# Attention and rational feed-forward on one core: float32 products with undivided w_out in the first twelve units, w_out divided later, denominators added by GpSimd throughout

## The chip, the cores and the metric

The kernel runs on one core of one Trainium2 chip. The metric is device time in microseconds of one execution, measured over several runs; one further execution was recorded by the hardware profiler. The engines are called as the profile calls them: PE (TensorE matmuls), PEld (its weight loads), DVE (VectorE), ACT (ScalarE), POOL (GpSimd), SP (SyncE, which issues the transfers).

## The reference

```python
# q, k, v: 8 x 8 x 576 x 64; p: 8 x 8 x 32 x 64 (batch, head, row, head_dim)
def sm_attn(qq, kk, vv):
    s = scale * np.matmul(qq, kk.transpose(0, 1, 3, 2))
    s = s - np.max(s, axis=-1, keepdims=True)
    a = np.exp(s)
    a = a / (np.sum(a, axis=-1, keepdims=True) + 1e-09)
    return np.matmul(a, vv)
p_packed = sm_attn(p, k, v)
x = sm_attn(q, p_packed, p_packed)      # then to 4608 rows of 512 = 8 heads x 64
# w_in: 512 x 2048, w_out: 2048 x 512, both given in float64; a: 4, b: 2 numbers
h = x @ w_in
P = a[0] + a[1] * h + a[2] * h2 + a[3] * h3
Q = 1.0 + np.abs(b[0]) * np.abs(h) + np.abs(b[1]) * h2
g = P / (Q + 1e-6)
out = (g @ w_out).astype(np.float32)    # 4608 x 512
```

## The kernel before

**Units.** The feed-forward part runs in 128 units: 8 batches, two halves `x` of a batch's 576 rows, and 8 chunks `c` of 256 of the 2048 hidden columns. `hidden(bb, x, c)` makes a unit's hidden values in two halves `f` of 128 columns: six matmuls into an `h` bank, then the numerator `Y` (ACT, then two instructions of DVE), the denominator `U`, its reciprocal by Ln and Exp on ACT and a correction on DVE, and the quotient `g` in `Y`. It is a generator with four parts, and step `u` of the main loop runs the first two parts of unit `u`, the last of unit `u-2` and the third of unit `u-1`. The rows of a half are 256 (`HMAIN`, multiplied unit by unit) and 32, which are gathered in `G` and multiplied by `remainder` for two batches together.

**Exactness by division.** Matmuls of full speed take `fp32r` operands, which hold fewer bits than float32. So `split` divides a float32 operand into a rounded part (an ACT cast, `gh`) and the rest (a POOL subtraction, `gl`), and a product is three matmuls: `gh` by `wh`, `gh` by `wl`, `gl` by `wh`, in `accumulate`. `acc_block(u, i)` multiplies a unit's 128-row part `i` by the chunk's two rows of w_out and adds it up in a PSUM bank over the eight chunks: 12 matmuls of 512 columns for a unit. It is called at step `u + 3` (`LAG`).

**Words.** w_in and w_out come as 64-bit words of float64. `load_words` brings a chunk into a free buffer (`room` lists the buffers and up to which word they may be used), and `convert` makes float32 of it: two ACT instructions and three on DVE (a mask by `TENSOR_SCALAR`, a shift by `SCALAR_TENSOR_TENSOR`, a 32-bit sum, which the profile calls `CUSTOM_DVE_ANT_0`). A chunk of w_out is then divided by `split` into `W[c]`, kept in the ring `w`: eight buffers of 8 KB in each partition, four parts of 512 columns each. The last chunk of w_out comes in two halves through the buffers `o` and `full`. Four words are converted before the main loop, then at least one in each step, so that `converted < len(words)` holds for units 0 to 9.

**Denominators.** While words are left (`early`), the denominator is made by ACT (`Abs`), DVE (a second product by `h`) and ACT again (`Abs` of the whole); later ACT makes `Abs` and `Square` (into `sq`, a ring of one buffer), and POOL adds the two.

**Order.** `Planner` records every operation with its engine and operands, finds the dependences, prices each operation (a float32 matmul at 30 ns and 1.667 ns a column, an fp32r one at 15 and 0.417), and issues all of them in the order of a list schedule. `idle` puts small matmuls on a zero tile between PE's operations, where that schedule leaves PE idle in its first 150 us; they add zeros to a sum that is open. In the profile all operations of the schedule have line 226, the zero matmuls line 223; so the tiles' names tell the operations apart. The next batch's `attention` and `m_chunk` (the packed keys times w_in) are spread over the steps as fillers.

Of the kernel before, what the change touches and what calls it, by code (L numbers as in the profile page):

```python
# [23 lines left out]
P = 128  # L24
# [233 lines left out]
def attention_rational_ffn(  # L258
# [46 lines left out]

    w_ring = Ring(sb, "w", NCH, [P, 2, 2, DM], F32R)
    o_ring = Ring(sb, "o", 1, [P, 2, DM])

# [51 lines left out]

    words = [("in", 2 * c, 2) for c in range(NCH)] + [("out", 2 * c, 2) for c in range(NCH - 1)]
    words += [("out", NFC - 2 + i, 1) for i in range(2)]
    due = lambda x: x[1] // 2 + (LAG if x[0] == "out" else -2)
# [3 lines left out]
    room = [((m_ring, i), index["in", 4 * i] + 1) for i in range(NCH // 2)]  # L367
    room += [((w_ring, c), index["out", 2 * c]) for c in range(1, NCH)]
    started = False
    words_in, converted = [], 0  # L370

    def load_words(n):
        while len(words_in) < min(len(words), converted + n):
            r = len(words_in)
            kind, i, n2 = words[r]
            used = [x for x, _ in words_in]
            free = [x for x, end in room if r < end and x not in used[converted:]]
            free = [x for x in free if x[0] is not w_ring or x[1] < NCH - 2 or started]
            if not free and r == converted and n2 == 1:
                free = [(o_ring, 0)]  # L380
            if not free:
                return
            x = min(free, key=lambda x: max((j for j in range(r) if used[j] == x), default=-1))
            raw = x[0].at(x[1], [P, n2 * 512], I64)
            if kind == "in":
                c = i // 2
                for y in range(2):
                    src = w_in[2 * y * P : (2 * y + 2) * P, c * CF : (c + 1) * CF].rearrange("(x p) f -> p x f", p=P)
                    nc.sync.dma_start(raw[:, 512 * y : 512 * (y + 1)].rearrange("p (x y) -> p x y", x=2), src)
            else:  # L390
                for y in range(n2):
                    nc.sync.dma_start(raw[:, 512 * y : 512 * (y + 1)], w_out[(i + y) * P : (i + y + 1) * P, :])
            words_in.append((x, raw))

    W = {}

# [4 lines left out]
    def convert():  # L401
# [9 lines left out]
        if kind == "in":  # L411
            dst = win[:, i // 2]
            di = dst.bitcast(I32)
        else:
            dst = lo.bitcast(F32)
            di = w_ring.at(i // 2, [P, n * DM], I32) if n == 2 else full_ring.next(dtype=I32)
            di = di.rearrange("p (x y) -> p x y", x=n)
        nc.scalar.activation(hi.bitcast(F32), hi.bitcast(F32), AF.Copy, scale=REBIAS)
# [4 lines left out]
        nc.vector.tensor_add(dst.bitcast(I32), hi, di)  # L423
        if kind == "out":
            if i // 2 not in W:
                W[i // 2] = w_ring.at(i // 2)
            for y in range(n):
                split(dst[:, y, :], *(W[i // 2][:, (i + y) % 2, x, :] for x in range(2)))
        converted += 1
# [14 lines left out]
    def load(bb, what):  # L444
# [43 lines left out]
        if bb == 0 and x != "k":  # L488
            if g == 0:
                NAT[x] = w_ring.at(NCH - 2 + "vq".index(x), [P, 2, 4 * NS * D], F32)  # L490
            t = NAT[x][:, g, :]
        else:
            t = nat_ring.next()[:, 0 : 4 * NS * D]
# [283 lines left out]

    def hidden(bb, x, c):
        ah, al = AH[bb], AL[bb]
        mh, ml = (M[bb, c // 2][:, i, :, c % 2 * CF : (c % 2 + 1) * CF] for i in range(2))  # L780
        early = converted < len(words)
        U, V, Y = U_ring.next(), V_ring.next()[:, :, 0:HALF], Y_ring.next()
        U2 = None if early else U2_ring.next()
        for f in range(2):
# [8 lines left out]
            nc.scalar.activation(y, h, AF.Identity, scale=reg_a3, bias=a2)  # L793
            nc.scalar.activation(u, h, AF.Abs, scale=reg_b1 if early else reg_b0)
            if not early:
                nc.scalar.activation(U2[:, f, :], h, AF.Square, scale=reg_root)
            nc.vector.tensor_mul(y, y, h)
            nc.vector.scalar_tensor_tensor(y, y, a1, h, ALU.add, ALU.mult)


            if early:
                nc.vector.scalar_tensor_tensor(u, u, b0, h, ALU.add, ALU.mult)
            elif f == 1:
                nc.gpsimd.tensor_add(U, U, U2)
            yield
        if early:
            nc.scalar.activation(U, U, AF.Abs)
        nc.scalar.activation(V, U, AF.Ln, bias=one)
        nc.scalar.activation(V, V, AF.Exp, scale=-1.0)
        nc.vector.scalar_tensor_tensor(Y, Y, a0, V, ALU.add, ALU.mult)  # L810
        nc.vector.scalar_tensor_tensor(V, U, (1.0 + 1e-6) * S, V, ALU.add, ALU.mult)
        yield
        nc.vector.scalar_tensor_tensor(Y, V, 2.0, Y, ALU.subtract, ALU.mult, reverse0=True)
        gh, gl = GS[bb, x, c] = gh_ring.next(), gl_ring.next()
        split(Y[:, :, 0:HMAIN], gh, gl)
        r0 = (bb % 2) * REM + x * HREM
        nc.gpsimd.tensor_copy(G[:, 2 * c : 2 * c + 2, r0 : r0 + HREM], Y[:, :, HMAIN:HALF])
        yield

    def accumulate(acc, gh, gl, fc, first, last):  # L820
        wh, wl = (W[fc // 2][:, fc % 2, x, :] for x in range(2))
        for i, (x, w) in enumerate(((gh, wh), (gh, wl), (gl, wh))):
            nc.tensor.matmul(acc, x, w, start=first and i == 0, stop=last and i == 2)
# [3 lines left out]
    def remainder(bb, f4):  # L827

        full = G[:, 4 * f4 : 4 * f4 + 4, :].rearrange("p a b -> p (a b)")
        gx = o_ring.next(dtype=F32R)  # L830
        gh, gl = gx[:, 0, :], gx[:, 1, :]
# [23 lines left out]
    def acc_block(u, i):  # L855
        bb, x, c = units[u]
        if c == 0 and i == 0:
            ACC[bb, x] = [acc_ring.next() for _ in range(2)]
        gh, gl = GS[bb, x, c]
        acc = ACC[bb, x][i]  # L860
        for f in range(2):
            cols = slice(i * P, (i + 1) * P)
            accumulate(acc, gh[:, f, cols], gl[:, f, cols], 2 * c + f, c == 0 and f == 0, c == NCH - 1 and f == 1)
        if c < NCH - 1:
            return
        if i == 0:
            O[bb, x] = o_ring.next()
        o = O[bb, x]
# [52 lines left out]
    for u in range(NU + LAG + 2):  # L921
# [23 lines left out]
    def idle(i, t0, t1):  # L945
# [47 lines left out]
```

## Time and profile before

| | us |
|---|---|
| median of the runs (lowest, highest of 3) | 802.2 (801.95, 803.88) |
| the profiled execution, its own time | 802.42 |
| its span, from first to last instruction | 800.6 |
| PE busy | 751.5 (94%) |
| DVE busy | 707.2 (88%) |
| ACT busy | 670.5 (84%) |
| POOL busy | 460.5 (58%) |

A share of busy time is an average over the whole span. The page also divides the span into 40 equal slices of 20 us, and any stretch can be asked for by itself. A group's row names the operation, the tiles it writes and reads, its shape and count, then busy microseconds, the mean of one in ns, and the idle time of the engine before it with what ended that. Matmuls overlap one another, so the mean of one is longer than its share of PE's time; how far apart they start tells the latter.

### The profile page before, as it was taken

What the parts mean: (1) busy time and instruction counts of PE and PEld (TensorE: products, weight loads), DVE (VectorE), ACT (ScalarE), POOL (GpSimd) and SP (SyncE); (2) the same over time, 40 slices, a digit from 0 to 9 for tenths busy, and PEclk for the clock granted to TensorE, in tenths of its full rate; (3) what the DMA queues carried; (4) which work ended last, traced back from release to release, by engine and by line L of the source; (5) the groups of instructions that cost most, each with busy time, mean ns of one, the idle gap of its engine ahead of it and who ended that gap; (6) DMA issues with size and microseconds to landing.
All of it is one profiled execution on the core that took longest, in us unless ns stands there. A gap on an engine that the chain in (4) does not pass through costs nothing.

```text
span 800.6 us, 15433 instructions
## 1 busy us (share of the span) xinstructions
PE 751.5 (94%) x5537; PEld 593.6 (74%) x5537; DVE 707.2 (88%) x1309; ACT 670.5 (84%) x1494; POOL 460.5 (58%) x462
## 2 busy tenths in 40 slices
PE   2767989999999999999999999999999999999997
PEld 1446667778878788778877888778877887778886
DVE  4599999998899799998899789998899789998883
ACT  4699989889888898889888798889788798998972
POOL 0003547755577555756568455855578555866663
PEclk9958999999999999999999999999999999999999
DMA  7983236010651109120720219020810123000001
GB/s 249 365 272 108 89 105 86 27 57 27 76 78 43 40 15 124 30 57 28 105 48 3 81 25 133 11 57 28 116 37 28 53 41 60 1 1 27 27 1 40
DMA packets 152029, 56.05 MB, mean 70 GB/s; under 512 B 122256, under 2 KB 141200, under 8 KB 151952
## 3 DMA queue, kind: packets, MB, share of 16 engines
q1 hardware_dynamic: 151952, 55.07, 30.4%
q8 instruction: 43, 0.70, 0.4%
q14 instruction: 34, 0.28, 0.1%
HBM read 45.62 MB, written 9.44 MB: 69 GB/s over the span
## 4 chain that ended last, share of the span: by engine, by line
PE 73%; DVE 14%; ACT 8%; issue 2%; DMA 2%; SPq 1%; POOL 0%; DVEq 0%; ACTq 0%
PE acc L226 37%; PE h L226 23%; PE at L226 13%; DVE Y L226 5%; DVE w L226 3%; DMA nat<-in_k_dram 2%; ACT Y L226 2%; DVE small L226 1%; ACT U L226 1%; DVE kx L226 1%; ACT V L226 1%; ACT sq L226 1%; DVE V L226 1%; ACT kx L226 1%; DVE win L226 1%
## 5 line engine op out<-in xcount | busy, mean ns | idle before, releaser
L226 PE MATMUL acc<-w,gh 128*128 128x512 f32 x1024 | 324.2, 399 | 3.8 <-ACT gh L226 2.2
L226 PEld LDWEIGHTS acc<-w,gh 128*128 128x128 f32 x1024 | 184.3, 188 | 53.8 <-issue 7.5
L226 POOL TENSOR_TENSOR U<-U,sq 128x576 f32<-128x576 f32 x118 | 168.9, 1431 | 82.1 <-ACT U L226 48.7
L226 PE MATMUL h<-AH,m 128*128 128x288 f32 x1024 | 189.0, 304 | 10.6 <-DVE Y L226 8.0
L226 POOL TENSOR_TENSOR gl<-Y,gh 128x512 fp32r<-128x512 f32 x128 | 165.9, 1296 | 50.1 <-ACT gh L226 22.2
L226 PE MATMUL acc<-w,gl 128*128 128x512 f32 x512 | 191.3, 396 | 0.0
L226 PEld LDWEIGHTS h<-AH,m 128*128 128x128 f32 x1024 | 158.2, 190 | 39.7 <-DVE Y L226 24.2
L226 ACT ACTIVATE Y<-h,abS 128x288 f32<-128x288 f32 x256 | 125.6, 508 | 17.8 <-PE h L226 13.3
L226 ACT ACTIVATE sq<-h 128x288 f32<-128x288 f32 x236 | 97.5, 415 | 41.0 <-PE h L226 31.8
L226 DVE TENSOR_TENSOR Y<-Y,h 128x288 f32<-128x288 f32 x256 | 109.5, 444 | 25.0 <-ACT Y L226 9.3
L226 DVE SCALAR_TENSOR_TENSOR Y<-Y,abS,h 128x288 f32<-128x288 f32 x256 | 124.8, 504 | 2.3
L226 DVE SCALAR_TENSOR_TENSOR Y<-Y,abS,V 128x576 f32<-128x576 f32 x128 | 102.9, 804 | 21.9 <-ACT V L226 21.5
L226 PEld LDWEIGHTS acc<-w,gl 128*128 128x128 f32 x512 | 96.0, 188 | 27.3 <-issue 8.0
L226 PE MATMUL h<-AL,m 128*128 128x288 f32 x512 | 110.9, 297 | 0.0
L226 ACT ACTIVATE U<-h 128x288 f32<-128x288 f32 x256 | 98.6, 420 | 11.1 <-DVE V L226 5.7
L226 ACT ACTIVATE V<-U,one 128x576 f32<-128x576 f32 x128 | 98.0, 765 | 6.4 <-DVE Y L226 6.2
L226 POOL COPY G<-Y 128x64 f32<-128x64 f32 x128 | 34.3, 268 | 115.8 <-DVE Y L226 103.3
L226 DVE SCALAR_TENSOR_TENSOR Y<-V,Y 128x576 f32<-128x576 f32 x128 | 95.4, 746 | 1.9
L226 DVE SCALAR_TENSOR_TENSOR V<-U,V 128x576 f32<-128x576 f32 x128 | 96.0, 750 | 0.0
L226 ACT CAST gh<-Y 128x512 fp32r<-128x512 f32 x128 | 81.0, 633 | 6.0 <-DVE Y L226 5.3
L226 ACT ACTIVATE V<-V 128x576 f32<-128x576 f32 x128 | 84.6, 661 | 0.5
L226 PEld LDWEIGHTS h<-AL,m 128*128 128x128 f32 x512 | 83.0, 190 | 0.1
(127 smaller groups left out, 856.2 us busy)
## 6 DMA issues: line engine op xcount, KB each, us to landing
out_dram<-o SPq DMA_DIRECT2D x15, 512.0 KB, 2.8
w<-in_moe_w_out_dram SPq DMA_DIRECT2D x14, 512.0 KB, 4.4
nat<-in_k_dram SPq DMA_DIRECT2D x48, 144.0 KB, 3.9
nat<-in_q_dram SPq DMA_DIRECT2D x48, 144.0 KB, 4.2
nat<-in_v_dram SPq DMA_DIRECT2D x24, 256.0 KB, 4.0
m<-in_moe_w_in_dram SPq DMA_DIRECT2D x8, 512.0 KB, 7.5
w<-in_moe_w_in_dram SPq DMA_DIRECT2D x8, 512.0 KB, 9.7
nat<-in_k_dram SPq DMA_DIRECT2D x4, 512.0 KB, 11.1
```

Source lines behind the costliest of these rows:

```text
L226: getattr(getattr(self.nc, engine), name)(*args, **kwargs)
```

## The change

Four things are changed.

- The first twelve units (`PLAIN`) multiply in float32: `g` isn't divided, it is written by DVE as float32, the 256 rows into a buffer of `gh` or `gl`, and the 32 straight into `G`; and `acc_block` makes four float32 matmuls by the undivided chunk `X[c]` instead of twelve. These are all eight chunks of the first half of batch 0 and four of the second.
- `convert` leaves a chunk of w_out undivided, in `X[c]`. `divide(c)` makes `W[c]` of it by one ACT cast of 1024 columns and two POOL subtractions, at steps 11, 12, 14, 15, 17, 18, 20 and 21.
- All units make the denominator by `Abs` and `Square` on ACT and a POOL addition.
- The buffers: `w` has six instead of eight, a ring `half` of five buffers of 4 KB takes undivided chunks 2 and 3, two divided ones and what was `o`; raw words use `m0` to `m3` and `w1` to `w5`; batch 0's `v` and `q` lie in `w2` and `w3` instead of `w6` and `w7`. The last chunk of w_out comes as one word like the others.

```diff
+    PLAIN = 12
+    UNDIVIDED = {0: (0, 1), 4: (4, 5), 5: (6, 7)}
+    DIVIDE = dict(zip((11, 12, 14, 15, 17, 18, 20, 21), (4, 5, 6, 7, 0, 1, 2, 3)))
+    DIVIDED = {4: 1, 5: 2, 6: 3, 7: 4, 0: 5, 1: (2, 3), 2: 0, 3: (0, 4)}
...
-    w_ring = Ring(sb, "w", NCH, [P, 2, 2, DM], F32R)
-    o_ring = Ring(sb, "o", 1, [P, 2, DM])
+    w_ring = Ring(sb, "w", NCH - 2, [P, 2, 2, DM], F32R)
+    half_ring = Ring(sb, "half", 5, [P, 2, DM])
...
-    words = [("in", 2 * c, 2) for c in range(NCH)] + [("out", 2 * c, 2) for c in range(NCH - 1)]
-    words += [("out", NFC - 2 + i, 1) for i in range(2)]
+    words = [(kind, 2 * c, 2) for kind in ("in", "out") for c in range(NCH)]
...
-    room += [((w_ring, c), index["out", 2 * c]) for c in range(1, NCH)]
+    room += [((w_ring, i), len(words)) for i in (1, 2, 3)]
+    room += [((w_ring, i), index["out", 2 * UNDIVIDED[i][0]]) for i in (4, 5)]
...
+    def divide(c):
+        place = DIVIDED[c]
+        if isinstance(place, int):
+            t = w_ring.at(place)
+            hi, lo = W[c] = t[:, 0], t[:, 1]
+        else:
+            hi, lo = W[c] = [half_ring.at(i, dtype=F32R) for i in place]
+        nc.scalar.copy(hi, X[c])
+        for f in range(2):
+            nc.gpsimd.tensor_sub(lo[:, f], X[c][:, f], hi[:, f].bitcast(F32))
+
+    def o_next(dtype=None):
+        return half_ring.at(1 if 3 in W else 4, dtype=dtype)
...
-            dst = lo.bitcast(F32)
-            di = w_ring.at(i // 2, [P, n * DM], I32) if n == 2 else full_ring.next(dtype=I32)
-            di = di.rearrange("p (x y) -> p x y", x=n)
+            dst = undivided(i // 2)
+            di = dst.bitcast(I32)
...
-        if kind == "out":
-            if i // 2 not in W:
-                W[i // 2] = w_ring.at(i // 2)
-            for y in range(n):
-                split(dst[:, y, :], *(W[i // 2][:, (i + y) % 2, x, :] for x in range(2)))
...
     def hidden(bb, x, c):
+        plain = (2 * bb + x) * NCH + c < PLAIN
...
-        early = converted < len(words)
-        U2 = None if early else U2_ring.next()
+        U2 = U2_ring.next()
...
-            nc.scalar.activation(u, h, AF.Abs, scale=reg_b1 if early else reg_b0)
-            if not early:
-                nc.scalar.activation(U2[:, f, :], h, AF.Square, scale=reg_root)
+            nc.scalar.activation(u, h, AF.Abs, scale=reg_b0)
+            nc.scalar.activation(U2[:, f, :], h, AF.Square, scale=reg_root)
...
-            if early:
-                nc.vector.scalar_tensor_tensor(u, u, b0, h, ALU.add, ALU.mult)
-            elif f == 1:
+            if f == 1:
                 nc.gpsimd.tensor_add(U, U, U2)
             yield
-        if early:
-            nc.scalar.activation(U, U, AF.Abs)
...
+        r0 = (bb % 2) * REM + x * HREM
+        if plain:
+            g = GS[bb, x, c] = (gh_ring if c % 2 == 0 else gl_ring).at(c // 2 % 2, dtype=F32)
+            for o, cols in ((g, slice(0, HMAIN)), (G[:, 2 * c : 2 * c + 2, r0 : r0 + HREM], slice(HMAIN, HALF))):
+                nc.vector.scalar_tensor_tensor(
+                    o, V[:, :, cols], 2.0, Y[:, :, cols], ALU.subtract, ALU.mult, reverse0=True
+                )
+            yield
+            return
...
     def acc_block(u, i):
...
+        if u < PLAIN:
+            for f in range(2):
+                g = GS[bb, x, c][:, f, cols]
+                nc.tensor.matmul(acc, g, X[c][:, f, :], start=c == 0 and f == 0, stop=c == NCH - 1 and f == 1)
+        else:
+            gh, gl = GS[bb, x, c]
+        for f in range(0 if u < PLAIN else 2):
             accumulate(acc, gh[:, f, cols], gl[:, f, cols], 2 * c + f, c == 0 and f == 0, c == NCH - 1 and f == 1)
...
+        if u in DIVIDE:
+            divide(DIVIDE[u])
...
-                n = min(args[0].shape[-1], 256)
+                n = min(args[0].shape[-1], 256 if args[1].dtype == F32R else 96)
```

More of the change, by code (lines that the diff above doesn't have):

```diff
@@ L377, in load_words @@
             free = [x for x, end in room if r < end and x not in used[converted:]]
-            free = [x for x in free if x[0] is not w_ring or x[1] < NCH - 2 or started]
-            if not free and r == converted and n2 == 1:
-                free = [(o_ring, 0)]
+            free = [x for x in free if x[0] is not w_ring or x[1] not in (2, 3) or started]
             if not free:
@@ L393, in load_words, with undivided @@
             words_in.append((x, raw))
-    W = {}
+    W, X = {}, {}
+    def undivided(c):
+        if c not in X:
+            pair = [i for i in UNDIVIDED if c in UNDIVIDED[i]]
+            if pair:
+                t = w_ring.at(pair[0], dtype=F32)
+                X.update({y: t[:, x] for x, y in enumerate(UNDIVIDED[pair[0]])})
+            else:
+                X[c] = half_ring.at(c - 2)
+        return X[c]
+    def divide(c):
[10 more added lines that the diff above has]
+        return half_ring.at(1 if 3 in W else 4, dtype=dtype)
     def split(x, hi, lo, eng=nc.gpsimd):
@@ L489, in load @@
             if g == 0:
-                NAT[x] = w_ring.at(NCH - 2 + "vq".index(x), [P, 2, 4 * NS * D], F32)
+                NAT[x] = w_ring.at(2 + "vq".index(x), [P, 2, 4 * NS * D], F32)
             t = NAT[x][:, g, :]
@@ L815, in hidden @@
         split(Y[:, :, 0:HMAIN], gh, gl)
-        r0 = (bb % 2) * REM + x * HREM
         nc.gpsimd.tensor_copy(G[:, 2 * c : 2 * c + 2, r0 : r0 + HREM], Y[:, :, HMAIN:HALF])
@@ L820, in accumulate @@
     def accumulate(acc, gh, gl, fc, first, last):
-        wh, wl = (W[fc // 2][:, fc % 2, x, :] for x in range(2))
+        wh, wl = (x[:, fc % 2, :] for x in W[fc // 2])
         for i, (x, w) in enumerate(((gh, wh), (gh, wl), (gl, wh))):
@@ L829, in remainder @@
         full = G[:, 4 * f4 : 4 * f4 + 4, :].rearrange("p a b -> p (a b)")
-        gx = o_ring.next(dtype=F32R)
+        gx = o_next(dtype=F32R)
         gh, gl = gx[:, 0, :], gx[:, 1, :]
@@ L858, in acc_block @@
             ACC[bb, x] = [acc_ring.next() for _ in range(2)]
-        gh, gl = GS[bb, x, c]
         acc = ACC[bb, x][i]
-        for f in range(2):
-            cols = slice(i * P, (i + 1) * P)
+        cols = slice(i * P, (i + 1) * P)
+        if u < PLAIN:
+            for f in range(2):
+                g = GS[bb, x, c][:, f, cols]
+                nc.tensor.matmul(acc, g, X[c][:, f, :], start=c == 0 and f == 0, stop=c == NCH - 1 and f == 1)
+        else:
+            gh, gl = GS[bb, x, c]
+        for f in range(0 if u < PLAIN else 2):
             accumulate(acc, gh[:, f, cols], gl[:, f, cols], 2 * c + f, c == 0 and f == 0, c == NCH - 1 and f == 1)
@@ L866, in acc_block @@
         if i == 0:
-            O[bb, x] = o_ring.next()
+            O[bb, x] = o_next()
         o = O[bb, x]
@@ L951, in idle @@
                 out, words = list(sums.values())[-1]
-                todo = [("matmul", (out, zero, words), dict(start=False, stop=False, skip_group_check=True))] * n
+                z = zero.bitcast(words.dtype)
+                todo = [("matmul", (out, z, words), dict(start=False, stop=False, skip_group_check=True))] * n
         for name, args, kwargs in nc.ops[i][1]:
             tag = str(args[0].tensor.tag)
-            if name == "matmul" and tag[:1] != "V" and tag[:2] != "at" and args[1].dtype == F32R:
+            if name == "matmul" and (tag[:1] == "h" or tag[:3] == "acc" and args[1].tensor.tag[:1] == "g"):
                 begun = begun or tag[:3] == "acc"
-                n = min(args[0].shape[-1], 256)
+                n = min(args[0].shape[-1], 256 if args[1].dtype == F32R else 96)
                 sums.pop(tag, None)
```

## The prediction

> **What bounds the kernel now.** I read the slices of the span first, then the chain, then the stages between the places where the slices change.
>
> ```profile
> PE   2767989999999999999999999999999999999997
> DVE  4599999998899799998899789998899789998883
> POOL 0003547755577555756568455855578555866663
> ...
> PE 73%; DVE 14%; ACT 8%; issue 2%; DMA 2%; SPq 1%; POOL 0%; DVEq 0%; ACTq 0%
> ...
> 45.00:75.00 30.00, 20.34 (x125) 15.52 (x126) 30.00 (x45) 27.45 (x53) 4.39 (x5) 0.67 0.57 171
> 75.00:145.00 70.00, 63.65 (x549) 48.21 (x547) 69.63 (x122) 63.39 (x135) 41.73 (x37) 1.00 0.38 88
> 145.00:205.00 60.00, 59.96 (x480) 47.67 (x480) 54.40 (x105) 52.95 (x125) 38.02 (x39) 1.00 0.12 37
> 205.00:795.00 590.00, 584.22 (x4131) 468.10 (x4130) 525.78 (x982) 497.97 (x1135) 375.33 (x376) 1.00 0.26 47
> ```
>
> The stage rows give busy microseconds of PE, weight loads, DVE, ACT and POOL, then clock and DMA. Two bounds follow each other. From 45 to 145 us DVE is busy 99.63 of 100 us: it converts the 64-bit words and computes the first units' nonlinearity. From 145 us on PE is busy 59.96 of 60 and then 584.22 of 590. So a microsecond of DVE taken out before 145 brings everything behind it forward, as long as PE follows; a microsecond of PE added after 145 is paid in full. The profiled execution took 802.42 us (span 800.6 and 1.8 around it), the median of the runs is 802.2; the sum is made against 802.4.
>
> **DVE before 145 us.** The ten units that run while words are left have a second product on DVE for the denominator. It goes; ACT squares and POOL adds in its place.
>
> ```profile
> L226 DVE SCALAR_TENSOR_TENSOR U<-U,abS,h 128x288 f32<-128x288 f32 x20 | 10.0, 501 | 0.3 <-ACT U L226 0.3
> ...
> 91.66 0.50 DVE L226 SCALAR_TENSOR_TENSOR U<-U,abS,h 128x288 f32<-128x288 f32 x1
> 92.09 0.50 DVE L226 SCALAR_TENSOR_TENSOR Y<-Y,abS,h 128x288 f32<-128x288 f32 x1
> ...
> L226 DVE TENSOR_SCALAR w<-w x11: 628/683/1819, 40.0 to 121.1; 128x1024 int32<-128x1024 int32 x11
> L226 DVE SCALAR_TENSOR_TENSOR w<-w x11: 1208/1212/2212, 42.6 to 122.4; 128x1024 int32<-128x1024 int32 x11
> L226 DVE CUSTOM_DVE_ANT_0 win<-w,win x4: 1158/1489/2322, 47.9 to 75.3; 128x2048 uint16<-128x2048 uint16 x4
> ...
> L226 DVE TENSOR_SCALAR w<-w 128x1024 int32<-128x1024 int32 x11 | 9.5, 874 | 0.0
> L226 DVE SCALAR_TENSOR_TENSOR w<-w 128x1024 int32<-128x1024 int32 x11 | 15.3, 1396 | 0.0
> L226 DVE CUSTOM_DVE_ANT_0 o<-o,full 128x1024 uint16<-128x1024 uint16 x2 | 2.3, 1148 | 0.0
> ...
> L226 POOL TENSOR_TENSOR w<-w,w 128x512 fp32r<-128x512 f32 x14 | 19.3, 1401 | 15.6 <-ACT w L226 8.1 <-issue 7.1 <-POOL gl L226 0.3
> L226 POOL TENSOR_TENSOR gl<-Y,gh 128x512 fp32r<-128x512 f32 x9 | 11.9, 1323 | 11.4 <-ACT gh L226 10.4 <-POOL G L226 1.0
> L226 POOL COPY G<-Y 128x64 f32<-128x64 f32 x10 | 6.4, 644 | 16.0 <-DVE Y L226 14.6 <-DVE small L226 1.4
> L226 POOL TENSOR_TENSOR w<-o,w 128x512 fp32r<-128x512 f32 x2 | 2.6, 1316 | 1.4 <-ACT w L226 1.4
> ```
>
> (1) Twenty products, each followed 0.43 us later by the next instruction (91.66 to 92.09): 20 x 0.43 = **-8.6**.
>
> (2) Word instructions sometimes take far longer than their median, up to 2.32 us. Against their medians the masks lose 11 x (874 - 683 ns) = 2.1 and the shifts 11 x (1396 - 1212) = 2.0; against their minima the four sums into win 2 x 331 + 1164 = 1.8 and the two into o, the shorter of 0.68, 2 x (1148 - 680) = 0.9. Together 6.8 us. These long ones lie on POOL's subtractions, as the pair here does on a POOL addition:
>
> ```profile
> 141.84 1.43 POOL L226 TENSOR_TENSOR U<-U,sq 128x576 f32<-128x576 f32 x1 [1.81 <-ACT U L226]
> 142.20 1.61 DVE L226 CUSTOM_DVE_ANT_0 o<-o,full 128x1024 uint16<-128x1024 uint16 x1
> ```
>
> POOL loses there 19.3 + 2.6 (words divided), 11.9 (gl) and 6.4 (G) = 40.2 us and gets ten additions of 1.43, 14.3 us. With less than half its work, I take half of the 6.8: **-3.4**. Ends: -6.8; and, if each of ten additions meets a word instruction as this one did (1.61 - 0.68 = 0.93), 9.3 - 6.8 = +2.5.
>
> Here the Trainium skill (GPSIMD Engine Reference, 1. Specifications) says that GpSimd shares its SBUF interfaces with VectorE and contends with instructions in a 2-port mode or with two SBUF inputs. The mask row, with one input in SBUF, fits the first half; the second half is weighed as a rival.
>
> (3) The last w_out chunk is converted as one word instead of two halves, three instructions fewer. One has a fixed cost: 288 elements take 501 ns and 1024 take 1212, so 0.97 ns each and 0.22 us beside, of which 0.15 are left where the next follows after 0.43: 3 x 0.15, about **-0.4**. (4) The last product of a plain unit is written in two pieces, an instruction more; 0 to 0.22 each, I take 0.1, ten before 145: **+1.0**.
>
> DVE: -8.6 - 3.4 - 0.4 + 1.0 = **-11.4**, between -14.8 and -5.5.
>
> **ACT, and what waits for POOL.** ACT is busy 63.39 of 70, so it could take DVE's place.
>
> ```profile
> L226 ACT ACTIVATE sq<-h 128x288 f32<-128x288 f32 x236 | 97.5, 415 | 41.0 <-PE h L226 31.8 <-POOL U L226 6.6 <-POOL G L226 1.2
> L226 ACT ACTIVATE U<-U 128x576 f32<-128x576 f32 x10 | 7.1, 713 | 0.0
> L226 ACT CAST gh<-Y 128x512 fp32r<-128x512 f32 x128 | 81.0, 633 | 6.0 <-DVE Y L226 5.3 <-PE acc L226 0.3
> L226 ACT CAST w<-w 128x512 fp32r<-128x512 f32 x14 | 9.0, 707 | 1.3 <-DVE w L226 1.3
> ```
>
> It gains 20 squares (8.3) and loses ten absolute values (7.1), nine casts of gh (5.7) and 16 casts of w (11.3): -15.8 us there, no bound. Now Ln waits for a POOL addition, and ACT's next squares wait for it too, since sq has one buffer; POOL is lightly loaded, so nothing is added. The chain to the product loses gh and gl (0.63 + 1.3 us): cover enough. SP: the same bytes of w_out go out in 16 issues; the raw words have rooms w1 to w5 instead of w1 to w7, and two of these wait for batch 0's v and q, with batch 1's loads queued behind. They land 6.2 us after issue in the median:
>
> ```profile
> DMA to landing us min/median/max: 3.5/6.2/11.5
> ```
>
> The mask row has 11 words from 40.0 to 121.1 us, one in 8, and three to four rooms are ahead: nothing. Without that cover one late word would cost up to 6.2.
>
> **PE.** A unit's twelve fp32r products become four float32 ones.
>
> ```profile
> 169.29 1.02 PE at L226 x16
> 176.92 2.78 PE acc L226 x12
> ...
> L226 PE MATMUL at<-win,ppT x576: 376/589/632, 37.7 to 704.0; 64*32 64x512 f32 x149, 64*32 64x256 f32 x43
> L226 PE MATMUL acc<-w,gh x1024: 387/393/525, 74.9 to 795.6; 128*128 128x512 f32 x171
> ...
> 75.00:145.00 70.00, 38.31 (x188) 27.39 (x187) 0.00 (x0) 0.00 (x0) 1.00 0.38 88
> ...
> L223 PE MATMUL acc<-w,zero 128*64 128x256 f32 x97 | 14.9, 284 | 0.0
> 135.61 1.58 PE L223 MATMUL acc<-w,zero 128*64 128x256 f32 x12
> 144.56 0.49 PE L226 MATMUL acc<-w,gh 128*128 128x512 f32 x1 [1.48 <-ACT w L226]
> ```
>
> The nearest float32 row: eight products of 512 columns, side by side on parts of the array and each in two instructions, last 1.02 us as a group (upper end, a product at full price). Of an fp32r product's 0.39 us only 0.23 are paid in a row (2.78 / 12), the other 0.16 is latency; without it 0.86, the lower end. I take 0.88, near the lower end because these stand in a row too. A unit: 4 x 0.88 - 2.78 = **+0.74** (0.66 to 1.30).
>
> The Trainium skill (FP8 and Floating Point Precision, TensorE Precision Notes) counts four passes for true FP32; at 0.23 us a pass that would be 0.93 a product, an estimate that adds 0.2 to a unit and about 0.8 to the sum below.
>
> Where it is paid: in 75 to 145 the acc row counts 188 products, 97 of them fillers (on zeros, into open sums): 91 real ones, 7.6 units. Units 0 to 7 pay 8 x 0.74 = 5.9 there, under cover: PE idles 70 - 63.65 = 6.35, and fillers, issued only where the plan has PE idle, take 97 x 0.12 (12 in 1.58) = 11.6; 18.0 free. The last wait ended by a divided word (144.56) goes as well. But 11.4 of shortening and 5.9 of products leave less than one microsecond of the 18, helped by an earlier start (unit 0 no longer waits for gh and gl, 2 us). So PE cannot follow wholly: I charge **+2.0** (0 to 7). Units 8 to 11 are multiplied after 145: 4 x 0.74 = **+3.0** (2.6 to 5.2).
>
> **The division, units 11 to 21.** Eight chunks: an ACT cast of 1024 columns (two of 0.71 at most, 1.4) and two POOL subtractions of 1.3 each, with three units' gh, gl and G gone (0.63; 1.3 + 0.24). In 145 to 205 ACT goes from 52.95 to at most 52.95 + 11.3 - 1.9 = 62 of 60; POOL from 38.02 to 38.02 + 20.8 - 4.6 = 54 of 60. Both are covered only just; three of the eight can go early, when the last word is in and both engines have room. Busy time counts latency, so I take **+1.0** (0 to 10).
>
> Sum: -11.4 + 2.0 + 3.0 + 1.0 = -5.4: 802.4 - 5.4 = **797.0**.
>
> **The rivals.**
> (a) DVE yields more and PE follows: -14.8 + 3.0 = -11.8, 790.6. For: POOL's load halves. Against: the 18 us of PE room.
> (b) PE takes over before 145: only the idle 6.35 and half of the fillers' 11.6 can be used. 12.2 - 5.9 = 6.3 of gain, less 3.0 and 1.0: 800.1, no change. For: fillers stand in waits, which in-order PE may not shed. Against: many of those waits are for DVE.
> (c) Slower: POOL in units 12 to 21. gl ends just ahead of its product:
>
> ```profile
> 163.87 1.28 POOL L226 TENSOR_TENSOR gl<-Y,gh 128x512 fp32r<-128x512 f32 x1
> 165.57 0.40 PE L226 MATMUL acc<-w,gh 128*128 128x512 f32 x1
> ```
>
> 0.42 us lie between. If in each of eight units one subtraction of 1.3 stands ahead of gl, PE loses 8 x 1.3 = 10.4 instead of the 1.0: -11.4 + 2.0 + 3.0 + 10.4 = +4.0, 806.4. It decides from about 6.4 lost (five units). For: POOL at 54 of 60. Against: 6 us left, and a plan that prices POOL.
> (d) DVE instructions with two SBUF inputs stall while POOL works.
>
> ```profile
> L226 DVE SCALAR_TENSOR_TENSOR Y<-V,Y x128: 700/750/760, 69.2 to 787.5; 128x576 f32<-128x576 f32 x128
> L226 DVE SCALAR_TENSOR_TENSOR V<-U,V 128x576 f32<-128x576 f32 x11 | 8.3, 752 | 0.0
> ```
>
> Three groups like the second row (8.3 us in 145 to 205) are 42% of that stage; 16.2 us more POOL would cost 6.8: 803.8. Against: the longest of 128 took 760 ns, the median 750, whatever POOL did. The Trainium skill's section named at (2) states this contention; these rows do not bear it out.
>
> **How the numbers follow.** Forecast (793 to 800) 0.50, (a) 0.16, (b) 0.16, (c) 0.15, (d) 0.03. Here 0.3%, 2.4 us, is about what a measurement can tell from no change. Faster is the forecast and (a), 0.66; same (b) and (d), 0.19; slower (c), 0.15. 790 to 805 leaves out the worse half of (c) and the best of (a).
>
> **What would show it.** No U product on DVE, and word instructions near 0.68 and 1.21 us; PE solid from about 135 instead of 145; a float32 product in 0.86 to 1.02 us, 48 of them in two instructions each; fillers fewer; POOL near 54 of 60 and no PE idle on gl in the ten units after. Wrong would be: float32 products above 1.02 us, word instructions as long as before, PE solid before DVE has room, or PE waiting on gl or w between 140 and 210.

## The result, and the profile after

The changed kernel takes 795.88 us (median of four runs, 793.58 to 797.81) against 802.41 (801.95 to 803.88) of the kernel before on the same chip: a ratio of 0.992 with the interval 0.9904 to 0.9937, 6.5 us faster. Its profiled execution took 795.3 (span 793.2), 7.1 below the one before.

The slices and the chain of the changed kernel:

```profile
PE   2759999999999999999999999999999999999997
DVE  4698999998999889998999789998999789998873
POOL 0012357657576646756587556755587455856663
...
PE 76%; DVE 10%; ACT 10%; DMA 2%; issue 2%; SPq 1%; POOL 0%; DVEq 0%; ACTq 0%
```

PE's slices are full from the fourth on (about 60 us); before, but for the very last, the last one below 9 is the sixth (100 to 120 us). DVE's share of the chain falls from 14 to 10%. The stages (columns as before: start, end and length, then busy us of PE, weight loads, DVE, ACT and POOL, clock, DMA):

```profile
45.00:75.00 30.00, 22.79 (x127) 16.27 (x120) 27.46 (x41) 25.95 (x52) 4.26 (x3) 0.62 0.63 224
75.00:145.00 70.00, 68.62 (x527) 40.85 (x525) 67.76 (x128) 62.36 (x134) 36.82 (x26) 1.00 0.38 88
145.00:205.00 60.00, 60.00 (x464) 46.93 (x463) 54.97 (x105) 54.15 (x127) 39.70 (x40) 1.00 0.28 49
205.00:785.00 580.00, 573.27 (x4072) 458.20 (x4071) 519.15 (x967) 490.16 (x1119) 370.84 (x371) 1.00 0.25 45
```

PE's idle time in 75 to 145 went from 6.35 to 1.38 us; DVE, which had 0.37 us idle there and none in 45 to 75, now has 2.24 and 2.54. From 145 to 205 nothing is idle on PE. The last word's sum ends at 118.6 instead of 143.8, and the first product starts at 68.6 instead of 74.9.

The groups of DVE and POOL from 36 to 160 us (busy us and mean ns of one; then idle time before them); the first row is of the kernel before, the others of the changed kernel:

```profile
L226 DVE CUSTOM_DVE_ANT_0 win<-w,win 128x2048 uint16<-128x2048 uint16 x4 | 6.5, 1614 | 0.0
...
L226 DVE TENSOR_SCALAR w<-w 128x1024 int32<-128x1024 int32 x12 | 8.1, 684 | 0.3 <-ACT win L226 0.3
L226 DVE SCALAR_TENSOR_TENSOR w<-w 128x1024 int32<-128x1024 int32 x12 | 16.8, 1402 | 0.0
L226 DVE CUSTOM_DVE_ANT_0 win<-w,win 128x2048 uint16<-128x2048 uint16 x4 | 4.8, 1204 | 0.0
L226 DVE SCALAR_TENSOR_TENSOR gl<-V,Y 128x512 f32<-128x512 f32 x6 | 4.1, 679 | 0.0
L226 DVE SCALAR_TENSOR_TENSOR G<-V,Y 128x64 f32<-128x64 f32 x12 | 2.5, 211 | 0.0
L226 POOL TENSOR_TENSOR U<-U,sq 128x576 f32<-128x576 f32 x16 | 24.6, 1539 | 47.2 <-ACT sq L226 30.8 <-ACT U L226 13.1 <-DVE gh L226 3.2
L226 POOL TENSOR_TENSOR w<-w,w 128x512 fp32r<-128x512 f32 x10 | 13.7, 1387 | 5.5 <-ACT w L226 3.1 <-PE h L226 2.4
```

There is no product into U on DVE any more. The masks have come down from 874 to 684 ns and the four sums into win from 1614 to 1204; the shifts, at 1402, have not. The float32 products on PE, counted in halves (two instructions a product):

```profile
134.21 1.88 PE L226 MATMUL acc<-w,gh 128*128 128x512 f32 x4
146.71 3.59 PE L226 MATMUL acc<-half,gh 128*128 128x512 f32 x8
```

Four halves more are 1.71 us more, 0.43 a half and 0.86 a product.

To say where the time went I added up DVE's instructions of each kernel from 30 us to the end of `V<-U,V` of unit 16, where both kernels have left the words behind. "Collisions" is what instructions take above the fastest quarter of their own form in all kernels measured here; the other columns hold the rest of their time, by what they belong to ("unit" is Y, V and the like; a last group of 4.8 us in both is left out).

| us | end | idle | collisions | words | unit | U | attention |
|---|---|---|---|---|---|---|---|
| before | 182.0 | 4.9 | 9.4 | 37.8 | 62.8 | 8.6 | 23.8 |
| after | 173.8 | 7.2 | 5.4 | 37.6 | 64.6 | 0 | 24.3 |
| difference | -8.2 | +2.3 | -4.0 | -0.2 | +1.8 | -8.6 | +0.5 |

At the end of unit 16 the changed kernel is 8.2 us ahead, and at the end of the run 7.5: what DVE won is what the kernel won, and PE gave back less than one.

The runs below were measured on several chips, each beside the kernel before (802.35 to 803.04 us there). A difference between two changed kernels, taken from their medians, can therefore be off by more than 1 us. A changed order of the list schedule also moves the time; only e3, e4, e5 and e12 keep the order of the kernel they start from.

### The profile page after: what moved, and what is told of

It reads as the page before. It is cut to its first block, busy times and chain, and to the rows that moved or that the text cites. A ratio compares the mean times of both kernels' runs of the same rounds, so it can differ in the third digit from the quotient of the medians.

```text
span 793.2 us, 15205 instructions
## 1 busy us (share of the span) xinstructions
PE 751.6 (95%) x5452; PEld 578.9 (73%) x5452; DVE 698.0 (88%) x1298; ACT 662.4 (84%) x1482; POOL 453.3 (57%) x448
## 4 chain that ended last, share of the span: by engine, by line
PE 76%; DVE 10%; ACT 10%; DMA 2%; issue 2%; SPq 1%; POOL 0%; DVEq 0%; ACTq 0%
PE acc L226 38%; PE h L226 23%; PE at L226 14%; DVE Y L226 5%; DVE w L226 2%; ACT Y L226 2%; ACT U L226 1%; DMA AH<-in_k_dram 1%; ACT m L226 1%; ACT kx L226 1%; ACT V L226 1%; ACT sq L226 1%; DVE small L226 1%; DVE V L226 1%; ACT w L226 1%
## 5 line engine op out<-in xcount | busy, mean ns | idle before, releaser
L226 POOL TENSOR_TENSOR U<-U,sq 128x576 f32<-128x576 f32 x128 | 184.9, 1445 | 117.9 <-ACT U L226 54.6
L226 PE MATMUL acc<-w,gh 128*128 128x512 f32 x736 | 237.6, 408 | 1.5 <-ACT gh L226 1.0
L226 POOL TENSOR_TENSOR gl<-Y,gh 128x512 fp32r<-128x512 f32 x116 | 150.1, 1294 | 43.3 <-issue 18.0
L226 PEld LDWEIGHTS acc<-w,gh 128*128 128x128 f32 x736 | 132.1, 188 | 44.8 <-issue 12.2
L226 PE MATMUL acc<-w,gl 128*128 128x512 f32 x384 | 148.1, 413 | 0.7 <-DVE gl L226 0.7
L226 ACT ACTIVATE sq<-h 128x288 f32<-128x288 f32 x256 | 106.1, 416 | 38.5 <-PE h L226 32.0
L226 DVE SCALAR_TENSOR_TENSOR Y<-V,Y 128x576 f32<-128x576 f32 x116 | 86.7, 748 | 1.8
L226 PEld LDWEIGHTS acc<-w,gl 128*128 128x128 f32 x384 | 71.5, 188 | 22.7 <-issue 8.8
L226 POOL COPY G<-Y 128x64 f32<-128x64 f32 x116 | 27.5, 237 | 97.6 <-DVE Y L226 87.0
L226 PE MATMUL acc<-half,gh 128*128 128x512 f32 x240 | 78.6, 414 | 1.1 <-ACT gh L226 1.1
```

What stands on the lines that cost most here:

```text
L226: getattr(getattr(self.nc, engine), name)(*args, **kwargs)
```

## Each half of the change alone

**e1_pool_alone** is the kernel before with the denominators of all units added up by POOL; nothing else is changed. **e2_products_alone** is the changed kernel with the old denominators while words are left.

```diff
-        early = converted < len(words)      # e1: kernel before
+        early = False
```
```diff
-        U2 = U2_ring.next()                 # e2: changed kernel
+        early = converted < len(words)
+        U2 = None if early else U2_ring.next()
...
+            if early:
+                nc.vector.scalar_tensor_tensor(u, u, b0, h, ALU.add, ALU.mult)
...
```

> The kernel before with one part of the change alone: the denominators of all units are added by POOL; products, division and words stay. Own theory (DVE before 145 us is what the change relieves): DVE loses 20 x 0.43 = 8.6 us, POOL gets 14.3 us beside the 40.2 it keeps, so collisions with word instructions grow from 6.8 by about 2.4; 802.4 - 6.2 = 796.2 (794 to 799). Rival A (the gain lies in the float32 path, whose products start 6 us earlier and free ACT and POOL): 801 to 805, as much as POOL's own chain may cost.

> The changed kernel with the old denominators (DVE and ACT) while words are left: float32 products and late division alone. Own theory: POOL before 145 us is nearly empty, collisions 6.8 mostly gone, -0.4 and +1.0 as predicted, +3.0 for units 8 to 11, +1.0 for the division: 802.4 - 6.2 + 4.0 = 800 (798 to 804). Rival A: nearly the whole gain, 795 to 798. Rival B (PE is bound from its first product on, so each float32 unit costs its 0.9 us): 803 to 808.

Measured: e1 810.97 (before 803.04), ratio 1.0097 [1.0081, 1.0112]: 8 us slower, outside both of its ranges. e2 800.64, ratio 0.9968 [0.9955, 0.998]: 2.4 faster, in the range of the own theory. The two alone add up to a loss of 5.5 us; together they gain 6.5. In e1, DVE is rid of the product into U and is 9.4 us ahead at unit 4, but DVE loses it again: the ledger has 13.4 us of idle time and 14.2 of collisions (4.9 and 9.4 before). What is late can be seen in the sequence of e1's instructions on PE and POOL (start, length, and in brackets idle time and what ended it):

```profile
128.74 0.73 PE L226 MATMUL acc<-w,gh 128*128 128x512 f32 x2 [2.45 <-ACT w L226]
151.80 0.73 PE L226 MATMUL acc<-w,gh 128*128 128x512 f32 x2 [1.01 <-ACT w L226]
...
135.04 1.30 POOL L226 TENSOR_TENSOR w<-o,w 128x512 fp32r<-128x512 f32 x1 [1.97 <-ACT w L226]
136.37 0.35 SPq L226 DMA_DIRECT2D o<-in_moe_w_out_dram  x1
```

PE waits for divided words, and the last half of w_out can be loaded only after POOL has subtracted out of the buffer `o` at 135.04 to 136.34; its sum ends at 151.1 instead of 143.8.

## Is it the last half word?

The theory was then that this chain (POOL's subtraction, load of the last half, its division, the product) sets the time. **e10_no_last_half** is the kernel before without the last half word, **e11_pool_no_last_half** is e1 without it, and **e9_last_in_halves** is the changed kernel with the last chunk in two halves again, both through one buffer of 4 KB, each loaded only when the word before it is converted.

```diff
-    words += [("out", NFC - 2 + i, 1) for i in range(2)]      # e10, e11
+    words += [("out", NFC - 2, 1)]
...
-            for y in range(n):
-                split(dst[:, y, :], *(W[i // 2][:, (i + y) % 2, x, :] for x in range(2)))
+            for y in range(2):
+                split(dst[:, y % n, :], *(W[i // 2][:, y, x, :] for x in range(2)))
```
```diff
-    words = [(kind, 2 * c, 2) for kind in ("in", "out") for c in range(NCH)]      # e9
+    words = [("in", 2 * c, 2) for c in range(NCH)] + [("out", 2 * c, 2) for c in range(NCH - 1)]
+    words += [("out", NFC - 2 + i, 1) for i in range(2)]
...
+            if n2 == 1:
+                free = [(half_ring, 4)] if r == converted else []
...
-            dst = undivided(i // 2)
+            dst = undivided(i // 2)[:, i % 2 : i % 2 + n]
```

> The kernel before, with the last half word of w_out neither loaded nor converted (the first half of that chunk takes its place in the sums; work of all engines but SP, ACT and DVE stays, DVE loses 1.5 us). New theory: PE no longer waits at 140.04 to 144.56; 802.4 - 4 to 6 = 796.5 to 798.5. Old theory (DVE work bounds): 802.4 - 1.5 = 801.

> The kernel with POOL's additions alone (810.97), with the same last half word left out. New theory: with the chain gone, the 8.6 us saved on DVE show: 794 to 798. Rival D (POOL itself, with divided words, gl, G and additions, is what makes that kernel late): 804 to 809.

> The changed kernel with one part undone: the last w_out chunk comes again in two halves through one buffer of 4 KB, the second loaded only when the first is converted. New theory (the serial chain of the last half word, from its load at 131.7 to its use on PE at 144.56 in the kernel before, is what the early stage ends on; one word instead of two takes it away): the last chunk is converted 10 us later or more, and unit 7's product waits: 795.9 + 3 to 6 = 799 to 802. As predicted before (fixed costs only): 795.9 + 0.4 = 796.3.

Measured (before 802.82): e10 803.86, ratio 1.0016 [1.0005, 1.0028]; e11 800.74, 0.9973 [0.9961, 0.9984]; e9 795.6, 0.9916 [0.9903, 0.9929]. So the chain costs nothing in the changed kernel: e9 is where after is, as the fixed costs alone said, and the new theory's 799 to 802 was wrong. Where POOL carries everything, the half word costs 10 us (e11 against e1), though e11 hit neither of its ranges. With the chain gone, the additions alone are worth 3.1 us (e11 against e10). Each of these two pairs compares different orders.

What the chain costs in the kernel before stays open. e10 is no faster, though it converts half a chunk less, and missed both forecasts. But another order came out of the list schedule, and in it the 32-bit sums are longer. First a row of the kernel before (its win sums took 1614 ns), then two of e10, from 36 to 160 us:

```profile
L226 DVE CUSTOM_DVE_ANT_0 w<-w,w 128x2048 uint16<-128x2048 uint16 x7 | 8.5, 1213 | 0.0
```
```profile
L226 DVE CUSTOM_DVE_ANT_0 w<-w,w 128x2048 uint16<-128x2048 uint16 x7 | 10.1, 1445 | 0.0
L226 DVE CUSTOM_DVE_ANT_0 win<-w,win 128x2048 uint16<-128x2048 uint16 x4 | 7.1, 1766 | 0.0
```

Collisions in the ledger are 13.8 us there, 9.4 in the kernel before. These 4.4 us could hide a gain of that size.

## Collisions of word instructions with POOL

**e12_before_no_sub** keeps the kernel before in its own order and drops only POOL's sixteen subtractions that divide w_out, at the moment of issue; the products take the rounded part in place of the missing one. **e5_no_sub** does the same with the sixteen subtractions of the changed kernel.

```diff
+            nc.alt[len(nc.ops) - 1] = []      # behind nc.gpsimd.tensor_sub of w_out
...
-            for name, args, kwargs in calls:
+            for name, args, kwargs in self.alt.get(i, calls):
...
+            nc.alt[len(nc.ops) - 1] = [("matmul", (acc, x, wh), dict(start=first and i == 0, stop=last and i == 2))]
...
```

> The kernel before in its own order, with POOL's 16 subtractions of the words left out (the products with the rest of w_out use the rounded part instead, so PE does the same work). Collision theory (DVE's word instructions stall while POOL works): five of its eight long word instructions lie on these subtractions, 0.92 + 1.16 + 0.62 + 1.14 + 0.46 = 4.3 us over the median; 802.4 - 4.3 = 798.1 (797 to 800). If only the number of DVE's instructions counts: 802 to 803.

> The changed kernel in its own order, with the 16 subtractions of the division left out (PE does the same work on the rounded part instead). As predicted, the division costs 1.0, and one collision of 0.8 with a word at 92 us goes: 795.9 - 1 to 2 = 794 to 795. Rival (c), POOL overloaded in units 12 to 21: 788 to 792.

Measured (before 802.35): e12 798.48, ratio 0.9954 [0.9938, 0.9969], 3.9 faster than the kernel before; e5 793.44, 0.9886 [0.9869, 0.9902], 2.4 below after. e12 lies in the range of the collision theory, e5 0.6 below that of its own. The same instruction in the traces of the kernel before (first two rows) and of e12 (its line is one further down):

```profile
59.60 3.04 POOL L226 TENSOR_TENSOR w<-w,w 128x512 fp32r<-128x512 f32 x2 [7.29 <-ACT w L226]
61.40 2.32 DVE L226 CUSTOM_DVE_ANT_0 win<-w,win 128x2048 uint16<-128x2048 uint16 x1
```
```profile
59.99 1.21 DVE L227 CUSTOM_DVE_ANT_0 win<-w,win 128x2048 uint16<-128x2048 uint16 x1
...
L227 DVE TENSOR_SCALAR w<-w 128x1024 int32<-128x1024 int32 x11 | 7.5, 691 | 0.0
L227 DVE CUSTOM_DVE_ANT_0 win<-w,win 128x2048 uint16<-128x2048 uint16 x4 | 5.3, 1313 | 0.0
```

2.32 us under a subtraction, 1.21 without: the sum itself is unchanged. Here the cost is shown, not argued: the order is kept, and where POOL's subtraction is gone, the word instruction that lay on it is short. The shifts, at 1374 ns in e12, are still long on other work of POOL. In the ledger e12 has about 5 us less of collisions and 0.9 more of idle time than the kernel before, and its unit 16 ends 4.1 us earlier, so the gain is that of the collisions.

The rows also show what a collision is: DVE waits. POOL ends at 62.64 us (59.60 + 3.04) and the sum at 63.72 (61.40 + 2.32), 1.08 later, and alone it takes 1.21. In the traces of all fourteen kernels, 102 word instructions behind 36 us began while a POOL instruction had begun before them and had 0.1 us or more to go; 96 of them ended after POOL's end by their own time less 0.10 to 0.15 us, like this one. Of 52 that began before the POOL instruction that they overlap, 51 took their own time. A collision thus costs about what is left of POOL's instruction, and nothing to DVE where DVE is first.

Counted over all word instructions (mask, shift, sum) of a kernel, from the traces: how many overlap a POOL instruction by more than 0.3 us, what they lose (reckoned as in the ledger), and POOL's busy time from 45 us to the last word.

| kernel | words on POOL | lost, all | lost on POOL | POOL busy |
|---|---|---|---|---|
| before | 15 of 40 | 6.9 | 6.7 | 46.5 |
| e12 | 10 of 40 | 3.4 | 3.2 | 24.7 |
| after | 8 of 37 | 3.3 | 3.2 | 23.5 |
| e5 | 5 of 37 | 1.6 | 1.5 | 12.9 |
| e1 | 20 of 40 | 9.2 | 9.1 | 66.6 |
| e10 | 14 of 37 | 8.7 | 8.6 | 36.3 |

Nearly all of the lost time lies on POOL, and 0.11 to 0.15 us is lost for each microsecond in which POOL works while words are converted, 0.24 in the unlucky order of e10; over all fourteen kernels it is 0.09 to 0.24. All three kinds stall: the mask, which reads one tensor, and the shift and the sum, which read two, all in SBUF. For the shift and the sum the trace agrees with the contention that the Trainium skill states (GPSIMD Engine Reference, 1. Specifications). That the mask runs in the 2-port mode, which the section also names, no run here shows.

## What the additions are worth on POOL, and whether POOL could take more

**e8_dve_add** is the changed kernel with the additions on DVE while words are left; **e13_sums_on_pool** is the changed kernel with the 32-bit sums of w_out's words on POOL.

```diff
-                nc.gpsimd.tensor_add(U, U, U2)                               # e8
+                (nc.vector if converted < len(words) else nc.gpsimd).tensor_add(U, U, U2)
```
```diff
-        nc.vector.tensor_add(dst.bitcast(I32), hi, di)                       # e13
+        (nc.gpsimd if kind == "out" else nc.vector).tensor_add(dst.bitcast(I32), hi, di)
```

> The changed kernel with the additions of the units that run while words are left made by DVE (576 elements, 0.66 us each, some ten) instead of POOL. If DVE bounds up to about 160 us: 795.9 + 6.6 - up to 3.2 of collisions = 799 to 802.5. Rival B (PE bounds from its first product): 795.5 to 797.

> The changed kernel with the 32-bit sums of w_out's eight chunks made by POOL instead of DVE. Collision theory: DVE loses 8 x 1.13 = 9.0 us, POOL gets 8 x 2.4 = 19 us beside 42 before 145 us, collisions 5.4 x 19 / 42 = 2.4 more: 795.9 - 6.6 = 789, or 791 to 793 where PE, idle for 12 us before 145, does not follow. Rival (POOL's longer way to a word, and its queue, cost more than DVE gains): 797 to 802.

Measured: e8 799.91 (before 802.82), ratio 0.9965 [0.9951, 0.9979], 4 slower than after; e13 797.92 (before 802.35), 0.9948 [0.9933, 0.9962], 2 slower. e8 lies in the range for a bound by DVE; e13 missed the collision theory's 789 to 793 and lies in its rival's range. First a row of e8, then three of e13, all from 36 to 160 us:

```profile
L226 DVE TENSOR_TENSOR U<-U,sq 128x576 f32<-128x576 f32 x10 | 8.3, 826 | 0.0
```
```profile
L226 DVE SCALAR_TENSOR_TENSOR w<-w 128x1024 int32<-128x1024 int32 x12 | 19.1, 1588 | 0.0
L226 DVE TENSOR_SCALAR w<-w 128x1024 int32<-128x1024 int32 x12 | 11.9, 1002 | 0.6 <-ACT win L226 0.6
L226 POOL TENSOR_TENSOR half<-w,half 128x1024 int32<-128x1024 int32 (+1 forms) x4 | 7.3, 1844 | 7.5 <-ACT w L226 4.7 <-ACT half L226 2.8
```

Ten additions put back on DVE are 8.3 us of its time (6.6 of the ledger up to unit 16, since neighbours overlap); collisions (-0.8), idle time (-1.3) and the rest give a part of it back, and 2.9 us remain at unit 16. DVE still sets the time up to there. In e13 DVE has eight sums fewer, 8.9 us of words in the ledger (37.6 to 28.7), and loses almost all of it again: collisions go from 5.4 to 14.1, with the masks at 1002 ns and the shifts at 1588. At unit 16 it is 0.6 us ahead of after; at the end it is behind. That last part, 2 us, was not isolated.

## Is the float32 product paid for?

**e3_half_first8** drops one half of the float32 products of units 0 to 7 of the changed kernel at issue, **e4_half_last4** the same in units 8 to 11; the order of everything else is kept.

```diff
+                if u < 8 and f == (0 if c == NCH - 1 else 1):      # e3; e4: u >= 8
+                    nc.alt[len(nc.ops) - 1] = []
```

> The changed kernel in its own order, but units 0 to 7 issue only half of their float32 products (the other half is left out of the sums): 16 products, 16 x 0.86 = 13.7 us less PE work before about 133 us. Own theory (DVE bounds there, PE charged with 2.0): 795.9 - 2 = 794 (792 to 796). Rival B (PE is already the bound there, 68.6 of 70 us busy): 795.9 - 8 to 13, 783 to 788.

> The changed kernel in its own order, but units 8 to 11 issue only half of their float32 products (the other half is left out of the sums): 8 products, 8 x 0.86 = 6.9 us less PE work from about 134 to 158 us. Own theory and rival B (PE bounds there): 795.9 - 6.9 = 789 (788 to 791). Rival C (DVE, ACT or POOL still bounds while the chunks are divided): 793 to 796.

Measured (before 803.04): e3 794.38, ratio 0.9884 [0.9869, 0.9899]; e4 796.08, 0.9905 [0.9892, 0.9919]. e3 takes 16 products of 0.86, 13.7 us, off PE and is 1.5 us faster than after by the medians, 2.9 by the ratios; e4 takes 6.9 us off and is 0.2 us slower by the medians, 1.2 faster by the ratios, whose intervals overlap. e3 lies in the own theory's range; e4 missed the 788 to 791 of the own theory and rival B, and rival C's upper end, 796, is next to it. The stage in which e3 drops, then 125 to 165 us of after, then of e4:

```profile
75.00:145.00 70.00, 62.66 (x503) 38.28 (x503) 68.47 (x130) 62.48 (x136) 36.55 (x26) 0.98 0.37 88
```
```profile
125.00:145.00 20.00, 20.00 (x129) 10.22 (x127) 18.81 (x41) 17.81 (x37) 11.58 (x9) 1.00 0.60 79
145.00:165.00 20.00, 20.00 (x116) 12.91 (x114) 19.54 (x37) 18.98 (x43) 13.60 (x13) 1.00 0.01 2
```
```profile
125.00:145.00 20.00, 18.68 (x129) 9.58 (x128) 18.59 (x42) 18.16 (x41) 12.88 (x11) 1.00 0.65 86
145.00:165.00 20.00, 17.83 (x105) 11.80 (x106) 19.41 (x38) 18.78 (x42) 13.41 (x12) 0.91 0.00 1
```

What is taken off PE turns into idle time: 1.3 and 2.2 us of it in these two stretches of e4, while DVE is as busy as in after. These are all of PE's waits in e4 from 125 to 165 us, and the stretch behind the longest:

```profile
PE h L227 <- DVE Y L227: 3.5, 3, 2.2
...
150.00:155.00 5.00, 4.41 (x29) 2.73 (x29) 4.61 (x9) 3.78 (x10) 5.00 (x5) 0.66 0.00 0
```

PE waits for DVE's product `Y`, whereas DVE in the changed kernel waits for PE only once in 125 to 165, for 0.9 us. A PE that is 100% busy there thus doesn't set the time by itself; relieved, it waits for DVE, which is 19.54 of 20 busy. How little its work is worth is less certain than the time of e4 suggests: the clock granted in 150 to 155 us was 0.66 in e4 and 1.00 in after, up to 5 x 0.34 = 1.7 us of PE's work. In e4 DVE's unit 16 moved forward by 0.7 us against unit 0, and the end by no more; so 6.9 us off PE won 0.7, and by this estimate 2.4 at most.

## A version with eight such units

If DVE leads to about 165 us, the pieces of the last product that units 8 to 11 pay on DVE are for nothing, and the division can come earlier. **e6_plain8** makes eight units plain and divides the chunks in turn at units 9 to 16.

```diff
-    PLAIN = 12
-    UNDIVIDED = {0: (0, 1), 4: (4, 5), 5: (6, 7)}
-    DIVIDE = dict(zip((11, 12, 14, 15, 17, 18, 20, 21), (4, 5, 6, 7, 0, 1, 2, 3)))
+    PLAIN = 8
+    UNDIVIDED = {0: (0, 1), 4: (2, 3), 5: (4, 5)}
+    DIVIDE = dict(zip((9, 10, 11, 12, 13, 14, 15, 16), range(8)))
...
```

> The changed kernel with eight float32 units instead of twelve, the chunks placed so that the division runs at steps 9 to 16. If DVE bounds until about 160 us, as the run with half of the products of units 8 to 11 says, the 4 x 0.9 us of PE work are worth nothing and four more gh, gl and G (4 x 1.55 us of POOL) come back early: 796 to 799. Rival B (PE bounds): 792 to 793.

Measured (before 802.35): 791.34 (790.2 to 791.57), ratio 0.9858 [0.984, 0.9875], the fastest of all, and its interval lies clear of the changed kernel's. The own theory's 796 to 799 was missed, and the rival's 792 to 793 is nearer. But the rival's reason, less work on PE in units 8 to 11, doesn't fit the times: e6 is already 4.6 us ahead of after at the end of `V<-U,V` of unit 8, before any product of these units. Its words from 36 to 160 us, and its stages:

```profile
L226 DVE SCALAR_TENSOR_TENSOR w<-w 128x1024 int32<-128x1024 int32 x12 | 14.7, 1233 | 0.0
L226 DVE TENSOR_SCALAR w<-w 128x1024 int32<-128x1024 int32 x12 | 8.9, 745 | 0.3 <-ACT win L226 0.3
...
75.00:145.00 70.00, 68.66 (x539) 44.44 (x539) 67.98 (x126) 64.93 (x145) 39.87 (x32) 1.00 0.39 103
145.00:205.00 60.00, 58.94 (x479) 47.81 (x472) 56.27 (x109) 54.18 (x126) 44.28 (x45) 1.00 0.29 51
```

At the end of unit 16, with the division running from step 9, it is still 2.2 us ahead of after: 1.1 of it are collisions (the shifts at 1233 ns instead of 1402), 0.9 the pieces that four units no longer need, 0.3 idle time. Another 1.1 is won between units 22 and 24, where PE is full in both kernels and has four float32 units less behind it; that this is the cause is argued, not shown. The count of collisions is also a matter of the order that the schedule happens to give (e10 had the opposite luck), so the 1.1 us is not a sure gain of the edit.

## Why the prediction was right, and where it was right by luck

The time was predicted at 797.0 and is 795.88. By its own steps:

- **What bounds.** Right for the words; wrong in where DVE's bound ends. I put it at 145 us, because PE is 59.96 of 60 busy behind it. e4 shows DVE leading to about 165: a full PE that, relieved, waits for DVE.
- **(1) the product into U, -8.6.** Measured -8.6.
- **(2) collisions, -3.4.** Measured -3.6 in word instructions (6.9 to 3.3) and -4.0 in all. The reason given was POOL's halved load; POOL's busy time while words last did fall from 46.5 to 23.5 us. But it fell in another way than told: nine additions where ten were put, and six of the sixteen subtractions still before the last word, because words end at 118.6 and the division starts at 91.7. e12 and e5 then priced the subtractions alone at 3.9 us in the kernel before and 2.4 in the changed one.
- **(3) one word for two, -0.4.** Words came down by 0.2.
- **(4) pieces, +1.0.** Measured +1.8: too small, since the second piece has its own 211 ns row and twelve units have it.
- **ACT, and what waits for POOL: "nothing is added".** Here a term was missing. The longest of DVE's waits from 36 to 165 us in the changed kernel (before, there were three of 0.3 us each):

```profile
DVE Y L226 <- ACT V L226: 1.3, 1, 1.3
DVE kx L226 <- PE at L226: 1.2, 2, 0.9
DVE Y L226 <- ACT sq L226: 0.8, 2, 0.5
```

  DVE now waits for ACT, which it had done once, for 0.3 us; 2.3 us more idle time in the ledger. e2, without the early additions, idles more still (9.6), so it isn't POOL's longer way alone, and e9, the changed kernel in another order, idles 3.7; which part of the order it is stays open.
- **PE, a product of 0.88.** Measured 0.86, the lower end. The Trainium skill's four passes (FP8 and Floating Point Precision, TensorE Precision Notes) would, by the prediction's estimate, have made it 0.93; the measurement is lower.
- **PE, +2.0 for units 0 to 7.** Half of their products gone, 13.7 us, is worth 1.5 by the medians and 2.9 by the ratios (e3), so a charge of 2.0 for the 5.9 us that these units add isn't contradicted.
- **PE, +3.0 for units 8 to 11.** This is the term that failed: it takes 3.0 us as paid in full, and 6.9 us off the same products is worth 0.7, at most 2.4 (e4). It followed from the wrong end of DVE's bound.
- **Division, +1.0.** PE waits for no divided word and no subtraction in 75 to 205 us; these are all of its waits in the changed kernel:

```profile
PE acc L226 <- DVE gl L226: 0.7, 1, 0.7
PE acc L226 <- DVE gh L226: 0.5, 1, 0.5
PE at L226 <- DVE small L226: 0.2, 1, 0.2
```

  Its subtractions' price, 2.4 by e5, is paid elsewhere: in e5 DVE is 1.9 us ahead of after by unit 8 and stays there, with collisions down by 1.8. POOL stood at 39.70 in 145 to 205, not near 54, since twelve of the sixteen subtractions were over before.

So DVE yielded 8.2 instead of 11.4 (pieces 0.8 too little, idle time 2.3 and attention 0.5 left out, against 0.6 more from collisions), and PE took back 0.7 instead of 6.0 (what it cost before unit 16 would be in DVE's idle time, where waits for PE are 1.2 us, 0.3 before). The two errors nearly cancel, and the sum is right by 1.1 us; that closeness is luck. Of the rivals, (a) has PE follow, as it does, but DVE yielded less than it says; (b) and (c) are not seen in the rows. (d) doesn't come about in the rows that it priced: the 116 instances of `Y<-V,Y` in the changed kernel mean 748 ns:

```profile
L226 DVE SCALAR_TENSOR_TENSOR Y<-V,Y 128x576 f32<-128x576 f32 x116 | 86.7, 748 | 1.8
```

In the kernel before, those that overlap POOL take 740 ns in the mean and those that do not 750. But the prediction misread these rows as a test of two inputs in SBUF. `V` and `h` lie in PSUM, the memory that PE writes its sums to (`V_ring = Ring(ps, "V", ...)` in both kernels), so `Y<-V,Y` and `V<-U,V` read only one tensor from SBUF. An instruction that does read two is the float32 addition that e8 puts on DVE. One of its ten began under the first of two subtractions on POOL, which ended at 129.95 us:

```profile
128.66 3.04 POOL L226 TENSOR_TENSOR w<-w,w 128x512 fp32r<-128x512 f32 x2 [11.55 <-ACT w L226]
129.10 1.47 DVE L226 TENSOR_TENSOR U<-U,sq 128x576 f32<-128x576 f32 x1
```

The eight that met no work of POOL took 0.74 to 0.75 us. So for float32 instructions with two inputs in SBUF the trace agrees with what the Trainium skill (GPSIMD Engine Reference, 1. Specifications) states, as it does for the shifts and sums of the words. (d) costs nothing here because the units' products read PSUM.

What the prediction hadn't seen at all is that its parts don't add up: the additions on POOL are worth 8 us of loss in the old kernel (e1), 3 of gain without the late half word (e11 against e10, in two orders), and 4 of gain in the new one (e8).

## What to carry to other kernels

An engine at 100% is not yet the bound: before a microsecond on it is charged in full, ask whether its work would leave idle time behind if half of it went, and which engine the other then waits for. Work moved to an engine that idles isn't free if the busy one has to wait for its instructions to end: here each microsecond of GpSimd during the word conversion cost VectorE 0.09 to 0.24 us, so the cheapest place for it is after the last instruction that waits in this way. And a part of a change can lose by itself and gain with the rest, so test it with the rest in place.

## What the runs showed of the hardware that was not expected

Masks, shifts and 32-bit sums of 1024 columns on DVE (0.68, 1.21 and 1.21 us) take up to 2.48, 3.06 (both in e13) and 2.43 us (in e1) while POOL works, because they wait for POOL's instruction to end; products that read `V` or `h` from PSUM show nothing. Small float32 instructions wait as well: in the kernel before, `small<-small` of 18 columns (`TENSOR_SCALAR`) takes 0.16 us alone and 0.60 in the mean where it overlaps POOL. POOL suffers too: its `U<-U,sq` takes 1.54 us in the mean up to 160 us and 1.43 in 145 to 205 us of the changed kernel, and in the kernel before a copy into `G`, 0.24 us alone, took 2.90 at 122.50 us, when DVE had begun a shift 0.14 us before it. And a float32 product of 512 columns costs 0.86 us where three fp32r ones of 0.23 cost 0.69, so the float32 product is only a quarter dearer on PE than the divided one, and needs no division of its operands.
